# A transformer block on one core: the opening rearranged, empty matmuls as events of the schedule, a new rule table

## Chip, core and metric

The kernel runs on one core of a Trainium2 chip. The metric is the device time of one execution in microseconds (us); less is better. A core has TensorE (PE; its weight loads are listed as PEld), VectorE (DVE), ScalarE (ACT), GpSimd (POOL) and SyncE (SP), which issues most of the DMA transfers.

## The reference, cut to what matters

One block of 2048 tokens with 512 features: modulated layer norm, attention with 32 heads of 16 features, a residual, a second modulated layer norm, a gated FFN with 1792 hidden features, a residual.

```python
mod = (_silu(c) @ w_mod).reshape(c.shape[0], 6, 1, -1)
sa, ca, ga, sb, cb, gb = (mod[:, i].copy() for i in range(6))
h = _layernorm(x) * (1 + ca) + sa
q, k, v = split(h @ wqkv)                       # 32 heads of 16
p = _softmax(einsum('bhqd,bhkd->bhqk', q, k) * 16 ** -0.5)
x = x + ga * ((p @ v) @ wo)
h = _layernorm(x) * (1 + cb) + sb
x = x + gb * (_gelu(h @ w_gate) * (h @ w_up) @ w_down)
```

The scores are 32 x 2048 x 2048 elements, and each of them needs an exponential.

## The kernel before, in words

**The unit of work.** A slot is one bank of scores in PSUM, 128 partitions by 512 columns; the whole softmax has 2048 slots. Four heads are worked on together, on four groups of 32 partitions of TensorE. The queries are cut into seven sets (512, 512, 256, 256, 256, 128 and 128 columns), and a set and a group of four heads are a unit. The variable `pos` counts slots as they are given out.

**Who takes the exponential.** ScalarE takes two or three slots in one instruction (tile `ps_sc` in, tile `E` out, line 399). VectorE takes the others in quads of four slots: it writes bits that are a first approximation of the power of two (`bits`, line 1311: one TENSOR_SCALAR of 512 columns from `ps_sc` per slot), and then makes two factors of them with two masks and one product over 2048 columns each (`power_task`, line 1572). A quad's slots go either one at a time as the third bank beside two of ScalarE's, or three at once with no ScalarE slot beside them ("alone").

**The order of the work** is made when the program is built. A planner keeps a model of every engine's free time and picks what PE does next: scores for the next exponential, products with v, or a piece of side work (projections, output projection, FFN, in a list with due positions). VectorE's work that comes of it waits in a list of tasks, whose length is `backlog()`. Whatever the planner decides becomes the fixed order of instructions on each engine; semaphores do the rest. What steers it are nine numbers for every 64 slots of `pos` (`RULES`, line 69, one row for each stretch, `SEGB = 64`):

- `ready`: how far ahead of PE's modelled time an operation may become ready and still be taken now
- `hole`: how long VectorE may stand empty before a slot until another task is put there
- `back`: the backlog from which no new quad is opened (line 1300)
- `fill`: the columns of PE work in the last 3413 ns below which an empty matmul is put into a gap
- `early`: how late VectorE may be for a quad's slot beside ScalarE's to be accepted (line 1471)
- `alone`: ScalarE's backlog from which three slots go to VectorE alone (line 1453)
- `lag`: the debt from which side work goes first
- `ahead`: the distance in `pos` of the next candidate for a quad
- `side2`: the debt from which side work gets a second PSUM bank, which is asked only from `pos` 1792 on

An empty matmul (`fillers`, line 1407) computes something that is overwritten or adds zeros. It is put in where PE would have a gap of more than 213 ns and its recent work is under `fill`, if one of the possible fillers is ready at once; otherwise the model's clock jumps to the next event.

**The opening** (`prologue`, line 582) is written by hand. DMA brings x, c, the first 1024 columns of w_mod in two parts and the weights of the first heads. The silu of c comes from a Tanh on ScalarE, four tiles of 128 tokens get mean and variance (`ln_stat` on VectorE; tile 1 on ScalarE with accumulating instructions), `ln_rstd` takes eight small VectorE steps for the reciprocal root of all four (tile `nwx`, `nwt`, `rstd`), and the tiles are normed into `dreg`, by VectorE (0 and 2) and ScalarE (1 and 3). `mod_cols` (line 725) computes the modulation as columns: columns 0 to 3 are the shift, 4 to 7 the scale, into `modA`. PE transposes the normed tiles into PSUM, `modulate` multiplies and adds on the way to `hreg`, and q and k of the first heads are projected. This goes in two halves of 256 tokens. k is masked into `kme` and `kmo` (even and odd heads), q is scaled into `qT`, and the first scores follow. Between the steps stand empty matmuls (`warm_up`, line 674).

**After the stream** a tail (line 1664) finishes the last two sets.

Of the kernel before, what the change touches and what calls it, by code (L numbers as in the profile page):

```python
# [6 lines left out]
ACT = mybir.ActivationFunctionType  # L7
ALU = mybir.AluOpType
BF16 = mybir.dt.bfloat16
# [5 lines left out]
P = 128  # L15
# [6 lines left out]
NDC = D // P  # L22
# [15 lines left out]
SC = 2 * CH  # L38
# [14 lines left out]
def WIN(ends):  # L53
# [8 lines left out]
URGENT = 12  # L62
TAILPV = -99
# [431 lines left out]
class _Kernel(_Recorder):  # L495
# [86 lines left out]
    def prologue(self):  # L582
        sp, act, pe, dve, pool = "sp", "act", "pe", "dve", "pool"
# [36 lines left out]
        self.act(self.tcol[:, :], self.scp[:, 0, 0:NDC], ACT.Tanh, scale=0.5)  # L620
        self.ln_stat(0)
# [4 lines left out]
        self.ln_stat(2)  # L626
        self.stt(self.tcol[:, :], self.tcol[:, :], 1.0, self.scp[:, 0, 0:NDC], ALU.add, ALU.mult)
        self.ts(dve, self.sc_bf[:, :], self.tcol[:, :], 0.5, None, ALU.mult)
        self.warm_up(10)
        self.mod_cols(self.scp[:, 1, 0:8], 0, 0, range(4))  # L630
        self.warm_up(8)
        self.ln_stat(3)
        self.ln_rstd(0, 4)
        nb = self.nwt[:, 0:4]
        self.stt(nb, self.mv[:, 0:4, 0], -1.0, self.rstd[:, 0:4], ALU.mult, ALU.mult)
        for t in (0, 1, 2, 3):
            dst = self.tb1[:, 0, t, :]
            if t % 2 == 0:
                self.ln_norm(t, dst)
            else:  # L640
                self.act(dst, self.xs[:, t, :], ACT.Identity, bias=nb[:, t:t + 1], scale=self.rstd[:, t:t + 1])
        self.copy(dve, self.modA[:, 0:4], self.scp[:, 1, 0:4])
        qb = [self.scp[:, 0, 0:256], self.scp[:, 1, 0:256]]
        kb = [self.pv[:, 0:256], self.scp[:, SC - 1, 0:256]]
        own = ((0, 0, 0, 1), (0, 0, 1, 1))
        pts = []
        for h in range(2):
            tb = [self.scp[:, 2 + 2 * h, :].bitcast(BF16), (self.mi if h else self.scp[:, 3, :])[:, :].bitcast(BF16)]
            pts.append([tb[own[h][dc]][:, 256 * dc:256 * dc + 256] for dc in range(NDC)])
            for i in range(2):  # L650
                for dc in range(NDC):
                    self.transpose(pts[h][dc][:, P * i:P * i + P], self.tb1[:, 0, 2 * h + i, P * dc:P * dc + P], self.ident[:, :])
            if h == 0:
                self.mod_cols(self.scp[:, 0, 0:8], 0, 0, range(4, 8))
        self.ts(dve, self.modA[:, 4:8], self.scp[:, 0, 4:8], 1.0, None, ALU.add)
        for h in range(2):
            hs = slice(256 * h, 256 * h + 256)
            for dc in range(NDC):
                self.modulate(act if own[h][dc] else dve, self.hT[:, dc, hs], pts[h][dc], self.modA, dc)
            for n, dc in enumerate((0, 3, 1, 2) if h == 0 else (2, 0, 3, 1)):  # L660
                for out, col in ((qb[h], 0), (kb[h], 512)):
                    self.mm(out, self.wqkv[:, dc, col:col + P], self.hT[:, dc, hs], start=(n == 0), stop=(n == NDC - 1))
        self.ts(dve, self.km[0][:, 0, 0:P], kb[0][:, 0:P], self.rm[:, 0:1], None, ALU.mult)
        self.ts(dve, self.qT[:, 0, 0:256], qb[0], Q_SCALE, None, ALU.mult)
        self.act(self.qT[:, 0, 256:512], qb[1], ACT.Copy, scale=Q_SCALE)
        self.ts(dve, self.km[0][:, 0, P:256], kb[0][:, P:256], self.rm[:, 0:1], None, ALU.mult)
        self.ts(dve, self.km[0][:, 0, 256:512], kb[1], self.rm[:, 0:1], None, ALU.mult)
        for h in range(2):
            self.ts(dve, self.km[1][:, 0, 256 * h:256 * h + 256], kb[h], self.rm[:, 1:2], None, ALU.mult)
# [554 lines left out]
    def stream(self):  # L1224
# [198 lines left out]
        while cg <= group[units[-1]]:  # L1423
# [7 lines left out]
            t = max(self.pe_now(), virt)  # L1431
# [12 lines left out]
            if tq is not None and tq <= t + self.rule.ready:  # L1444
# [41 lines left out]
                n = len(mem)  # L1486
# [345 lines left out]
```

## Time and profile before

| | us |
|---|---|
| median of 3 runs | 817.96 (816.5 to 818.49) |
| the profiled execution | 816.2 |
| its span, first to last instruction | 814.5 |
| ScalarE busy | 792.9 |
| VectorE busy | 753.7 |
| PE busy | 747.7 |

A row of a group reads: line, engine, operation, tile written <- tiles read, shape, count | busy time, mean ns of one | idle time of the engine just before, and what ended it. A row of the timeline reads: start, length, engine, line, operation, tiles, shape, count, and in brackets the idle time before and what ended it. Instructions that follow each other in the same form are merged into one row. A group's mean counts the overlap of neighbours twice, its busy time does not.

### The profile page before, as it was taken

How to read it: one execution, taken by the hardware profiler on the slowest of the kernel's cores; microseconds unless marked ns; L12 is line 12 of the kernel's file. 1: busy time of each engine (PE TensorE's matmuls, PEld its weight loads, DVE VectorE, ACT ScalarE, POOL GpSimd, SP SyncE). 2: the span in 40 equal slices, each digit the busy share in tenths (PEclk: the TensorE clock that was granted, in tenths of full speed). 3: DMA queues.
4: the chain of work that ended last, by engine and by line, in shares of the span. 5: the costliest groups of instructions: out<-in, count | busy, mean ns of one | idle time of the engine just before them, and what ended most of it. 6: DMA issues, size and time to landing. Idle time of an engine off the chain costs nothing.

```text
span 814.5 us, 30576 instructions
## 1 busy us (share of the span) xinstructions
PE 747.7 (92%) x13864; PEld 301.4 (37%) x13864; DVE 753.7 (93%) x1374; ACT 792.9 (97%) x743; POOL 4.6 (1%) x13
## 2 busy tenths in 40 slices
PE   8999999888998988899988989999999998999998
PEld 3333332322222222222233333333544344356565
DVE  7877999999999999999999999999999999889675
ACT  6999999999999999999999999999999999999993
POOL 2000000000000000000000000000000000000000
PEclk9999999999999999999999999999999999999999
DMA  8101000000002211110003212110644143330000
GB/s 285 54 15 23 9 11 9 7 12 10 2 9 63 83 48 36 41 49 21 16 18 99 61 49 58 45 36 10 177 129 135 51 134 101 85 103 9 20 10 14
DMA packets 77356, 43.73 MB, mean 54 GB/s; under 512 B 21285, under 2 KB 75626, under 8 KB 77226
## 3 DMA queue, kind: packets, MB, share of 16 engines
q1 hardware_dynamic: 77224, 41.78, 18.3%
q8 instruction: 108, 1.77, 0.9%
q14 instruction: 22, 0.18, 0.1%
q10 hardware_dynamic: 2, 0.00, 0.0%
HBM read 39.15 MB, written 2.60 MB: 51 GB/s over the span
## 4 chain that ended last, share of the span: by engine, by line
ACT 83%; PE 11%; DVE 5%; DMA 1%; issue 0%; SPq 0%; DVEq 0%
ACT E L399 79%; PE ps_sc L380 5%; PE ps_mi L380 4%; ACT hreg L399 2%; DVE mreg L411 2%; PE ps_pv L380 2%; ACT L399 1%; DVE dreg L411 1%; DMA mreg<-in_w_mod_dram 1%; DVE mreg L403 1%; DVE hreg L403 0%; DVE hreg L420 0%; DVE wo L430 0%; DVE wreg L411 0%; DVE hreg L411 0%
## 5 line engine op out<-in xcount | busy, mean ns | idle before, releaser
L399 ACT ACTIVATE E<-ps_sc 128x1024 bf16<-128x1024 f32 (+1 forms) x702 | 746.4, 1290 | 2.9 <-PE ps_sc L380 2.7
L380 PE MATMUL ps_sc<-qT,kmo 32*128 32x256 bf16 (+2 forms) x1728 | 197.5, 293 | 24.9 <-ACT E L399 21.2
L380 PE MATMUL ps_sc<-qT,kme 32*128 32x256 bf16 (+2 forms) x1728 | 194.4, 293 | 19.8 <-ACT E L399 16.2
L411 DVE TENSOR_SCALAR mreg<-ps_sc 128x512 uint16<-128x512 f32 x252 | 167.9, 683 | 11.4 <-PE ps_sc L380 9.5
L380 PE MATMUL ps_pv<-E,vaug 128*17 128x256 bf16 (+2 forms) x2720 | 150.0, 291 | 1.3 <-DVE osb L427 0.4
L411 DVE TENSOR_SCALAR dreg<-ps_sc 128x512 uint16<-128x512 f32 x160 | 106.9, 684 | 9.5 <-PE ps_sc L380 8.5
L380 PE MATMUL ps_mi<-wreg,mreg 128*32 128x256 bf16 (+2 forms) x1904 | 108.1, 326 | 4.1 <-DVE hreg L403 1.7
L380 PEld LDWEIGHTS ps_sc<-qT,kme 32*128 32x128 bf16 x1728 | 57.1, 92 | 138.5 <-ACT E L399 117.3
L380 PEld LDWEIGHTS ps_sc<-qT,kmo 32*128 32x128 bf16 x1728 | 58.1, 92 | 130.8 <-ACT E L399 113.2
L380 PEld LDWEIGHTS ps_pv<-E,vaug 128*17 128x17 bf16 x2720 | 53.9, 89 | 57.5 <-issue 41.1
L411 DVE TENSOR_SCALAR mreg<-mreg 128x2048 uint16<-128x2048 uint16 x100 | 67.8, 681 | 0.2
L380 PEld LDWEIGHTS ps_mi<-wreg,mreg 128*32 128x32 bf16 (+1 forms) x1904 | 42.2, 95 | 44.8 <-issue 18.5
L380 PE MATMUL ps_pv<-mreg,vaug 128*17 128x256 bf16 (+2 forms) x848 | 50.5, 298 | 2.8 <-DVE mreg L403 1.9
L403 DVE TENSOR_TENSOR mreg<-mreg 128x2048 bf16<-128x2048 bf16 x37 | 45.0, 1215 | 0.1
L403 DVE TENSOR_TENSOR mreg<-dreg,mreg 128x2048 bf16<-128x2048 bf16 x34 | 41.0, 1205 | 0.0
L380 PE MATMUL ps_mi<-hreg,wreg 128*32 128x512 bf16 x480 | 39.4, 385 | 0.8 <-DVE qT L411 0.5
L420 DVE CAST hreg<-ps_mi 128x512 bf16<-128x512 f32 (+1 forms) x49 | 33.0, 673 | 2.3 <-PE ps_mi L380 1.8
L380 PE MATMUL ps_mi<-wo,onorm 128*32 128x512 bf16 x448 | 34.2, 384 | 0.5 <-DVE onorm L403 0.5
L403 DVE TENSOR_TENSOR hreg<-ps_mi,hreg 128x512 bf16<-128x512 f32 x46 | 31.4, 682 | 1.0 <-PE ps_mi L380 0.7
L403 DVE TENSOR_TENSOR dreg<-mreg,dreg 128x2048 bf16<-128x2048 bf16 x26 | 31.4, 1210 | 0.0
L411 DVE TENSOR_SCALAR dreg<-dreg 128x2048 uint16<-128x2048 uint16 x46 | 31.1, 677 | 0.0
L380 PE MATMUL ps_mi<-mreg,hreg 128*32 128x512 bf16 x352 | 29.0, 385 | 0.0
(168 smaller groups left out, 677.6 us busy)
## 6 DMA issues: line engine op xcount, KB each, us to landing
mreg<-in_B_w_up_dram SPq DMA_DIRECT2D x32, 256.0 KB, 2.9
mreg<-in_B_w_gate_dram SPq DMA_DIRECT2D x28, 256.0 KB, 3.2
mreg<-in_B_w_down_dram SPq DMA_DIRECT2D x16, 256.0 KB, 2.7
dreg<-in_B_w_down_dram SPq DMA_DIRECT2D x12, 256.0 KB, 4.9
mreg<-in_w_mod_dram SPq DMA_DIRECT2D x1, 2048.0 KB, 12.1
rb<-scr_rec SPq DMA_DIRECT2D x64, 32.0 KB, 1.8
out_dram<-xs SPq DMA_DIRECT2D x15, 128.0 KB, 1.8
rb<-scr_rec SPq DMA_DIRECT2D x104, 16.0 KB, 1.7
```

What stands on the lines that cost most here:

```text
L380: return self.rec("pe", lambda e: e.matmul(out, lhsT, rhs, start=start, stop=stop, tile_position=tp), [lhsT, rhs, *after], [out], cost=(n, ...
L399: return self.rec("act", lambda e: e.activation(out, in_, func, scale=scale, **kw), rd, wr, cost=self.cost("act", out, [in_], "act") + load)
L403: return self.rec(eng, lambda e: e.tensor_tensor(out, a, b, op), [a, b], [out], cost=self.cost(eng, out, [a, b], "tt"))
L411: return self.rec(eng, lambda e: e.tensor_scalar(out, a, s1, s2, **kw), rd, [out], cost=self.cost(eng, out, [a], "ts") + (60 if len(rd) > ...
L420: return self.rec(eng, lambda e: e.tensor_copy(out, in_), [in_], [out], cost=self.cost(eng, out, [in_], "ts"))
```

## The change

In the opening:

- The statistics of tile 1 on ScalarE come before the Tanh. The three of VectorE come in one go, and the two small steps to the silu stand inside the chain of reciprocal roots.
- Behind the shift columns stand three empty matmuls instead of eight; the scale columns come after the transposes of tile 1 (`MODT = 1`) instead of after those of two tiles in the first half; two empty matmuls come before the projections.
- VectorE norms tiles 0, 1 and 3, ScalarE tile 2. ScalarE copies the shift.
- All four tiles are transposed before they are modulated, in 512 columns instead of two times 256, two on each engine.
- The first 128 key columns are projected apart from the other 384, and ScalarE masks them.

In the stream: of all fillers the one that is ready first is taken, and if none is ready at once, the moment at which it will be is one of the events to which the model's clock can jump. The rule table changes in 18 of its 32 rows: 0, 1, 2, 4, 10 to 14, 16, 18, 20, 23, 25, 26, 27, 30 and 31, in this order below.

```diff
+WARM = (3, 2)
+MODT = 1
 RULES = (
-    (80, 300, 8, 4200, 1536, 400, 1600, 20, 1800),
-    (80, 50, 8, 4200, 1536, 400, 1600, 20, 3200),
-    (60, 200, 7, 3900, 1536, 500, 1900, 24, 700),
+    (60, 200, 7, 3900, 1536, 500, 1600, 24, 700),
+    (80, 50, 10, 4200, 1536, 400, 1600, 20, 3200),
+    (60, 200, 7, 3900, 1536, 500, 1900, 24, 2500),
...
-    (30, 300, 8, 3900, 1536, 500, 2500, 24, 1800),
+    (110, 300, 8, 3900, 1536, 500, 3200, 24, 1800),
...
-    (80, 300, 8, 3600, 1536, 650, 3200, 20, 700),
-    (30, 300, 8, 3900, 1536, 650, 3200, 28, 1024),
-    (30, 200, 8, 3600, 2048, 500, 1300, 20, 1800),
-    (60, 50, 8, 3300, 768, 500, 1900, 12, 3200),
-    (80, 200, 8, 3300, 1536, 850, 3200, 12, 1024),
+    (60, 300, 8, 3600, 1536, 650, 3200, 20, 1800),
+    (30, 300, 8, 3900, 512, 650, 3200, 28, 1024),
+    (30, 50, 8, 3600, 2048, 500, 1300, 20, 3200),
+    (60, 50, 8, 4200, 768, 500, 1900, 16, 3200),
+    (45, 200, 8, 3600, 2048, 1100, 3200, 12, 1024),
...
-    (30, 300, 8, 3300, 1536, 850, 4000, 28, 3200),
+    (30, 300, 8, 3600, 1536, 850, 4000, 28, 3200),
...
-    (15, 200, 8, 3600, 2048, 500, 1900, 24, 2500),
+    (30, 200, 8, 3600, 1536, 850, 4000, 24, 1024),
...
-    (15, 200, 8, 3600, 2048, 500, 1600, 24, 3200),
+    (45, 200, 5, 3600, 2048, 500, 1600, 24, 3200),
...
-    (30, 50, 8, 4200, 768, 500, 3200, 20, 2500),
+    (30, 50, 8, 4200, 768, 500, 1900, 20, 2500),
...
-    (5, 50, 7, 4200, 2560, 850, 1900, 20, 700),
-    (80, 50, 10, 4200, 2560, 650, 1900, 20, 1800),
-    (5, 50, 10, 4200, 2048, 650, 1900, 20, 1800),
+    (110, 50, 7, 4200, 2560, 850, 1900, 20, 700),
+    (80, 50, 10, 4200, 2560, 650, 1600, 20, 2500),
+    (110, 50, 9, 4200, 2560, 850, 2500, 20, 700),
...
-    (80, 50, 10, 4200, 3500, 0, 1900, 20, 1800),
-    (80, 50, 11, 4200, 3500, 1100, 1900, 20, 1800),
+    (80, 50, 9, 3900, 3500, 0, 1900, 20, 1800),
+    (60, 50, 11, 4200, 3500, 300, 1900, 20, 1800),
 )
...
-        self.act(self.tcol[:, :], self.scp[:, 0, 0:NDC], ACT.Tanh, scale=0.5)
-        self.ln_stat(0)
...
-        self.ln_stat(2)
-        self.stt(self.tcol[:, :], ...)
-        self.ts(dve, self.sc_bf[:, :], self.tcol[:, :], 0.5, None, ALU.mult)
+        self.act(self.tcol[:, :], self.scp[:, 0, 0:NDC], ACT.Tanh, scale=0.5)
+        for t in (0, 2, 3):
+            self.ln_stat(t)
         self.warm_up(10)
+        for i in range(self.RSTD):
+            self.ln_rstd_step(0, 4, i)
+            if i == 2:
+                self.stt(self.tcol[:, :], ...)
+            elif i == 4:
+                self.ts(dve, self.sc_bf[:, :], self.tcol[:, :], 0.5, None, ALU.mult)
         self.mod_cols(self.scp[:, 1, 0:8], 0, 0, range(4))
-        self.warm_up(8)
-        self.ln_stat(3)
-        self.ln_rstd(0, 4)
+        self.warm_up(WARM[0])
...
+        for t in range(4):
+            for dc in range(NDC):
+                self.transpose(pts[dc][:, P * t:P * t + P], self.tb1[:, 0, t, P * dc:P * dc + P], self.ident[:, :])
+            if t == MODT:
+                self.mod_cols(self.scp[:, 0, 0:8], 0, 0, range(4, 8))
+        self.warm_up(WARM[1])
+        self.ts(dve, self.modA[:, 4:8], self.scp[:, 0, 4:8], 1.0, None, ALU.add)
...
+        kb = [self.pv[:, 0:P], self.scp[:, SC - 1, 0:512 - P]]
+        ks = [slice(0, P), slice(P, 512)]
+        for dc in range(NDC):
+            self.modulate(act if dc % 2 else dve, self.hT[:, dc, 0:512], pts[dc], self.modA, dc)
+            at = {"start": dc == 0, "stop": dc == NDC - 1}
+            self.mm(kb[0], self.wqkv[:, dc, 512:512 + P], self.hT[:, dc, ks[0]], **at)
+            for h in range(2):
+                self.mm(qb[h], self.wqkv[:, dc, 0:P], self.hT[:, dc, 256 * h:256 * h + 256], **at)
+        for dc in range(NDC):
+            self.mm(kb[1], self.wqkv[:, dc, 512:512 + P], self.hT[:, dc, ks[1]], start=(dc == 0), stop=(dc == NDC - 1))
+        self.act(self.km[0][:, 0, ks[0]], kb[0], ACT.Copy, scale=self.rm[:, 0:1])
         self.ts(dve, self.qT[:, 0, 0:256], qb[0], Q_SCALE, None, ALU.mult)
         self.act(self.qT[:, 0, 256:512], qb[1], ACT.Copy, scale=Q_SCALE)
+        for i, h in ((0, 1), (1, 0), (1, 1)):
+            self.ts(dve, self.km[i][:, 0, ks[h]], kb[h], self.rm[:, i:i + 1], None, ALU.mult)
...
-                fill = next((f for f in fillers() if self.probe(f) <= t + self.rule.ready), None)
+                fill = min([(self.probe(f), i, f) for i, f in enumerate(fillers())], default=None)
+                if fill is not None and fill[0] <= t + self.rule.ready:
+                    fill[2]()
+                    continue
                 if fill is not None:
-                    fill()
-                    continue
+                    nxt = min(nxt, fill[0])
             virt = nxt
```

More of the change, by code (lines that the diff above doesn't have):

```diff
@@ L625, in prologue @@
         self.act(self.mv[:, 1, 1:2], v1[:, 0:1], ACT.Copy, scale=1.0 / D)
-        self.ln_stat(2)
-        self.stt(self.tcol[:, :], self.tcol[:, :], 1.0, self.scp[:, 0, 0:NDC], ALU.add, ALU.mult)
-        self.ts(dve, self.sc_bf[:, :], self.tcol[:, :], 0.5, None, ALU.mult)
+        self.act(self.tcol[:, :], self.scp[:, 0, 0:NDC], ACT.Tanh, scale=0.5)
+        for t in (0, 2, 3):
+            self.ln_stat(t)
         self.warm_up(10)
+        for i in range(self.RSTD):
+            self.ln_rstd_step(0, 4, i)
+            if i == 2:
+                self.stt(self.tcol[:, :], self.tcol[:, :], 1.0, self.scp[:, 0, 0:NDC], ALU.add, ALU.mult)
+            elif i == 4:
+                self.ts(dve, self.sc_bf[:, :], self.tcol[:, :], 0.5, None, ALU.mult)
@@ L630, in prologue @@
         self.mod_cols(self.scp[:, 1, 0:8], 0, 0, range(4))
-        self.warm_up(8)
-        self.ln_stat(3)
-        self.ln_rstd(0, 4)
+        self.warm_up(WARM[0])
         nb = self.nwt[:, 0:4]
         self.stt(nb, self.mv[:, 0:4, 0], -1.0, self.rstd[:, 0:4], ALU.mult, ALU.mult)
-        for t in (0, 1, 2, 3):
+        for t in (2, 0, 1, 3):
             dst = self.tb1[:, 0, t, :]
-            if t % 2 == 0:
+            if t == 2:
+                self.act(dst, self.xs[:, t, :], ACT.Identity, bias=nb[:, t:t + 1], scale=self.rstd[:, t:t + 1])
+            else:
@@ L639, in prologue @@
                 self.ln_norm(t, dst)
-            else:
-                self.act(dst, self.xs[:, t, :], ACT.Identity, bias=nb[:, t:t + 1], scale=self.rstd[:, t:t + 1])
-        self.copy(dve, self.modA[:, 0:4], self.scp[:, 1, 0:4])
-        qb = [self.scp[:, 0, 0:256], self.scp[:, 1, 0:256]]
[L644 to L662, printed above, removed]
@@ L663, in prologue @@
-        self.ts(dve, self.km[0][:, 0, 0:P], kb[0][:, 0:P], self.rm[:, 0:1], None, ALU.mult)
+        self.act(self.modA[:, 0:4], self.scp[:, 1, 0:4], ACT.Copy)
+        tb = [self.scp[:, 2, :].bitcast(BF16), self.scp[:, 4, :].bitcast(BF16)]
+        pts = [tb[dc % 2][:, 512 * (dc // 2):512 * (dc // 2) + 512] for dc in range(NDC)]
+        for t in range(4):
[3 more added lines that the diff above has]
+                self.mod_cols(self.scp[:, 0, 0:8], 0, 0, range(4, 8))
@@ L668, in prologue @@
-        for h in range(2):
-            self.ts(dve, self.km[1][:, 0, 256 * h:256 * h + 256], kb[h], self.rm[:, 1:2], None, ALU.mult)
+        for i, h in ((0, 1), (1, 0), (1, 1)):
+            self.ts(dve, self.km[i][:, 0, ks[h]], kb[h], self.rm[:, i:i + 1], None, ALU.mult)
         self.ln_stat(4)
```

2 lines of the change are left out of this document (removed).

## The prediction

> **What bounds the kernel now.** I read the page first: span, busy time, the chain that ended last.
>
> ```profile
> span 814.5 us, 30576 instructions
> ...
> PE 747.7 (92%) x13864; PEld 301.4 (37%) x13864; DVE 753.7 (93%) x1374; ACT 792.9 (97%) x743; POOL 4.6 (1%) x13
> ...
> ACT 83%; PE 11%; DVE 5%; DMA 1%; issue 0%; SPq 0%; DVEq 0%
> ...
> L399 ACT ACTIVATE E<-ps_sc 128x1024 bf16<-128x1024 f32 (+1 forms) x702 | 746.4, 1290 | 2.9 <-PE ps_sc L380 2.7
> ```
>
> ScalarE holds 83% of the chain, and its exponentials alone are 746.4 of 814.5 us. All waiting ahead of those 702 instructions is 2.9 us, so nothing that merely feeds ScalarE better is worth more than that. Next I cut the span into stages.
>
> ```profile
> 0.00:14.40 14.40, 11.59 (x98) 5.95 (x98) 9.99 (x38) 6.46 (x13) 4.24 (x12) 1.00 0.83 249
> 14.40:43.40 29.00, 26.14 (x409) 9.65 (x412) 24.51 (x76) 28.57 (x25) 0.00 (x0) 1.00 0.32 114
> 43.40:68.70 25.30, 23.84 (x435) 8.87 (x435) 17.74 (x34) 25.18 (x25) 0.31 (x1) 1.00 0.08 23
> 68.70:700.00 631.30, 578.28 (x10048) 208.33 (x10044) 616.60 (x1038) 631.09 (x579) 0.00 (x0) 1.00 0.18 50
> 700.00:794.80 94.80, 91.89 (x2712) 57.13 (x2702) 74.05 (x162) 94.73 (x92) 0.00 (x0) 1.00 0.19 45
> 794.80:814.50 19.70, 15.92 (x199) 11.44 (x187) 10.79 (x32) 6.86 (x13) 0.00 (x0) 0.98 0.05 15
> ```
>
> Columns: length, then busy time of PE, PEld, DVE, ACT and POOL, the granted clock, DMA. The end of the kernel is 14.40 us of opening, 780.4 us in which ScalarE never rests (631.09 of 631.30 us in the long stage), and 19.70 us of tail. The change can move two of these: the moment of the first exponential, and how much of the softmax ScalarE has to do. VectorE does the rest of it, in fours ("quads"). It is 98% busy in the long stage (616.60 of 631.30) but idle 7.56 us of 25.30 in the stage before, and 20.75 of 94.80 in the last. The tail's code is not touched.
>
> **What one quad is worth.** From the groups by shape, for both engines:
>
> ```profile
> L399 ACT ACTIVATE E<-ps_sc 128x1024 bf16<-128x1024 f32 x458 | 450.1, 1149 | 0.6 <-PE ps_sc L380 0.5
> L399 ACT ACTIVATE E<-ps_sc 128x1536 bf16<-128x1536 f32 x240 | 349.2, 1573 | 0.6 <-PE ps_sc L380 0.6
> ...
> L411 DVE TENSOR_SCALAR mreg<-ps_sc 128x512 uint16<-128x512 f32 x252 | 167.9, 683 | 11.4 <-PE ps_sc L380 9.5
> L411 DVE TENSOR_SCALAR dreg<-ps_sc 128x512 uint16<-128x512 f32 x160 | 106.9, 684 | 9.5 <-PE ps_sc L380 8.5
> L411 DVE TENSOR_SCALAR mreg<-mreg 128x2048 uint16<-128x2048 uint16 x100 | 67.8, 681 | 0.2
> L403 DVE TENSOR_TENSOR mreg<-mreg 128x2048 bf16<-128x2048 bf16 x37 | 45.0, 1215 | 0.1
> ```
>
> A third slot of 512 columns costs ScalarE 1573 - 1149 = 0.424 us. ScalarE does 458x2 + 240x3 = 1636 slots, so the whole row of 746.4 us is 0.456 a slot. VectorE does 252 + 160 = 412 slots, 103 quads. One quad more takes 4 slots off ScalarE: 1.70 us by the slope, 1.82 by the average; I take 1.75. It costs VectorE four reads of PSUM at 167.9/252 = 0.666, two masks at 0.678 and one product at 1.216, together 5.2 us. Where VectorE has 5.2 us idle, a quad is a gain.
>
> **The opening, step by step.** The timeline from the vector c to the first exponential:
>
> ```profile
> 1.25 3.17 PE L380 MATMUL ps_mi<-dreg 128*128 128x512 bf16 x7 [1.25 <-DVE dreg L430]
> ...
> 4.55 2.36 PE L380 MATMUL ps_mi<-dreg 128*128 128x512 bf16 x10
> ...
> 4.65 0.17 ACT L399 ACTIVATE tcol<-ps_sc 128x4 f32<-128x4 f32 x1 [2.02 <-PE ps_sc L380]
> ...
> 5.33 0.15 DVE L416 SCALAR_TENSOR_TENSOR tcol<-tcol,ps_sc 128x4 f32<-128x4 f32 x1
> ...
> 5.59 0.68 DVE L442 BATCH_NORM_STATS2 st<-xs 128x6 f32<-128x512 bf16 x1
> ...
> 6.31 0.20 ACT L399 ACTIVATE mv<-nwx 128x1 f32<-128x1 f32 x1
> ...
> 6.62 0.17 DVE L411 TENSOR_SCALAR nwx<-mv 128x4 f32<-128x4 f32 x1
> ...
> 7.77 0.54 PE L380 MATMUL ps_sc<-sc_bf,mreg 128*128 128x1 bf16 x16 [0.86 <-DMA mreg<-in_w_mod_dram]
> ...
> 8.17 1.89 PE L380 MATMUL ps_mi<-dreg 128*128 128x512 bf16 x8
> ...
> 8.21 0.16 DVE L416 SCALAR_TENSOR_TENSOR nwt<-mv,rstd 128x4 f32<-128x4 f32 x1
> ...
> 8.29 0.73 DVE L411 TENSOR_SCALAR dreg<-xs,mv,rstd 128x512 bf16<-128x512 bf16 x2
> ...
> 9.90 0.61 PE L384 MATMUL ps_sc<-ident,dreg 128*128 128x128 bf16 x8
> ...
> 10.34 0.54 PE L380 MATMUL ps_sc<-sc_bf,mreg 128*128 128x1 bf16 x16
> ...
> 10.92 0.16 DVE L411 TENSOR_SCALAR modA<-ps_sc 128x4 f32<-128x4 f32 x1 [1.83 <-PE ps_sc L380]
> ...
> 11.77 1.04 DVE L411 TENSOR_SCALAR hreg<-ps_sc,modA 128x256 bf16<-128x256 bf16 x3
> ...
> 12.72 0.34 DVE L411 TENSOR_SCALAR kme<-ps_pv,rm 128x128 bf16<-128x128 f32 x1
> ...
> 13.44 0.38 ACT L399 ACTIVATE qT<-ps_sc 128x256 bf16<-128x256 f32 x1 [0.78 <-PE ps_sc L380]
> ...
> 13.96 0.59 PE L380 MATMUL ps_sc<-qT,kme 32*128 32x512 bf16 x5 [0.46 <-ACT qT L399]
> ...
> 14.40 10.49 ACT L399 ACTIVATE E<-ps_sc 128x1536 bf16<-128x1536 f32 x9 [0.58 <-PE ps_sc L380]
> ```
>
> *Statistics.* ScalarE now stands 2.02 us waiting for Tanh before it starts tile 1. With Tanh behind the tile's work, that starts at about 3.6 instead of 4.7, and the mean and variance of tile 1 are in about 1 us ahead of the rest. VectorE loses the two small steps in front of the third statistic (5.33 to 5.59, some 0.2 us), so the chain of reciprocal roots starts at about 6.35 instead of 6.62. The two small steps reappear inside the chain; eight steps fill 6.62 to 8.21, 0.2 us each, so they cost between 0 and 0.4, I take 0.2. Norms start about where they did (8.2 against 8.29). Gain: 0.1.
>
> *Matmuls between.* The first modulation columns wait for their weights (DMA, 7.77): unchanged. Behind them stand eight empty matmuls, 1.89 us, that hold the transposes until 9.90 although tile 0 is normed by 8.7 (8.29 and half of 0.73). Three of them are 0.7 us: transposes can start at 8.9. The scale columns now come after two tiles' transposes, at about 9.35. Their weights land in time:
>
> ```profile
> 2.32 0.51 SPq L452 DMA_DIRECT2D mreg<-in_w_mod_dram  x1
> ...
> mreg<-in_w_mod_dram SPq DMA_DIRECT2D x1, 512.0 KB, 6.8
> ```
>
> 2.32 + 6.8 = 9.1. So the scale columns run 9.35 to 9.9 and tiles 2 and 3 are transposed by about 10.5 (0.61 us for eight). Before, the first modulation was held by the scale until 10.92 + 0.16 = 11.1; now it is held by the last transpose, at about 10.6. Gain so far 0.55. The second pair of empty matmuls runs while VectorE and ScalarE modulate; that cover is about 0.5 us wide and without it they would cost 0.4.
>
> *Wide modulations.* Rows of the same operations at other widths:
>
> ```profile
> L411 DVE TENSOR_SCALAR hreg<-ps_mi,modA 128x512 bf16<-128x512 bf16 x12 | 6.0, 539 | 1.8 <-PE ps_mi L384 1.7
> ...
> L399 ACT ACTIVATE dreg<-xs,nwt,rstd 128x512 bf16<-128x512 bf16 x2 | 1.5, 806 | 1.9 <-DVE nwt L416 1.9
> ...
> L399 ACT ACTIVATE hreg<-ps_mi,modA 128x256 bf16<-128x256 bf16 x2 | 1.0, 558 | 0.0
> ```
>
> Four of 512 columns replace eight of 256. VectorE's pair ends at 10.6 + 2 x 0.54 - 0.1 of overlap = 11.6; ScalarE's is between 0.558 + 0.21 = 0.77 and 0.806 each, about 0.68 apart, and ends at 12.05. That is the last one; before, the last ends at 11.77 + 1.04 = 12.8. Gain so far 0.7.
>
> *Projections and first keys.* After the last modulation PE issues the 128-column key part and two query halves, and the second half is done at about 12.6. The price of putting the first 128 keys on ScalarE ahead of the second half of q: between 0 (it ends before the matmul that it would delay) and 0.34 us (VectorE's step of this shape at 12.72); I take 0.1. q is complete at about 13.1 against 13.44 + 0.38 = 13.82, the first scores start at 13.25, the first exponential at 13.7. The remaining 384 key columns are projected while ScalarE writes q, and masked on VectorE by 13.9, a second before the second exponential wants them. [...]
>
> Opening: 0.7 us earlier, between 0.2 (rsqrt chain dearer by 0.4, key step in the way) and 1.1 (none of these).
>
> **The stream.** The opening shifts the start of the stream, but the four key and query steps that VectorE still has there are nearly as long as before, so it gains little time by it; I count that as nothing. Fillers as events: a filler that becomes ready inside a gap is now issued there, and the gap's length is no longer skipped at once. PE is 92% busy and the granted clock 1.00 in every stage to 794.8, so more fillers buy no clock, and one too many costs its length, about 0.24 us (1.89/8), only where ScalarE's buffer of two exponentials has run dry; that is bounded by the 2.9 us of waiting. I take nothing for it.
>
> The rule table decides the number of quads. `side2` is asked only in the last four rules, where it stays as it was, so its edits do nothing. The others pull both ways: rule 1 lets a quad open with 10 steps in VectorE's backlog instead of 8, rules 14, 18 and 27 accept it with VectorE later by 200 to 350 ns, rules 23 and 26 start triples earlier; rule 20 lowers the backlog to 5, 27 and 30 by one, 31 cuts `early` from 1100 to 300, 4, 18 and 27 start triples later. In the long stage VectorE has 14.7 us idle in 631 (the windows above), in pieces; there I let the two signs cancel. Rule 1 acts in the stage 43.4 to 68.7, where idle time is in one place: 7.56 us, less the 0.7 us by which the stage comes earlier, divided by 5.2 is 1.3 quads, 1.3 x 1.75 = 2.3 us. A quad is whole, so one or two.
>
> Sum against the profiled execution: span 814.5 - 0.7 - 2.3 = 811.5. Its own time was 816.2, 1.7 over the span, so 813.2; the median of the runs, 817.96, lies 1.76 above the profiled one, so 815.0.
>
> **Rivals.** *Opening alone.* The backlog was not what held quads back in that stage; VectorE waits there for projections (PE ps_mi), and the count stays at 103. Against: nothing stronger than that rule 1 is the only edit with idle time under it. Time: 817.96 - 0.7 = 817.3, no measurable change.
>
> *Many quads.* The new rules and the last stage's 20.75 idle us hold three to six more: 812.0 down to 806.8. For: the idle time is there. Against: rules 30 and 31 are made stricter in that very stage.
>
> *Fewer quads, slower.* In the long stage rule 20's backlog of 5 and at the end rule 31's `early` turn away quads that were taken, since VectorE there is never short of backlog. Each costs ScalarE 1.75. It decides from two lost net: 817.96 - 0.7 + 3.5 = 820.8; four lost give 824.3. For: 98% busy with a backlog is the state in which a lower limit bites.
>
> *The clock.* In the opening PE loses 5 of 8 and gains 2 empty matmuls. The first seven at the kernel's start ran nearly half as fast (3.17 us for seven) as the next ten (2.36). If the clock fell back like that for some microseconds, half of the transposes (0.61) and the matmuls behind the last modulation (about 0.4) would lie on the path at twice their time: about 0.8 more, which eats the gain, 818.1. Against: the stretch from the three empty matmuls to the two is 1.6 us long (8.9 to 10.5) and has 16 transposes in it. [...]
>
> **Chances.** About 0.3% (2.5 us) is what a measurement of this kernel can tell from no change: 815.5 and 820.4 are the borders. Forecast, one or two quads, 0.44 (of it 0.34 below 815.5, 0.10 just above); many quads 0.16; opening alone 0.19; clock 0.04; fewer quads 0.17. Faster 0.34 + 0.16 = 0.50, same 0.10 + 0.19 + 0.04 = 0.33, slower 0.17. The range goes from four quads more (810.3) to two lost with 0.2 for an opening that gains less (821.0); five or six more, and three or more lost, some 0.13 together, stay outside. The forecast's own range is 813.5 to 816.
>
> **What would show it.** Right: first exponential between 13.3 and 14.2 us; first modulation near 10.6 held by a transpose; 104 or 105 quads (416 or 420 VectorE reads of ps_sc at 0.68); the stage after 43 us with under 5 us of VectorE idle; tail 19.7. Wrong: a first exponential at 14.4 or later, or more than 2 us of ScalarE waiting on PE inside the stream, or 101 quads or fewer.

## The result: 0.2% slower, and the profile after

The median of 22 runs each is 820.14 us after and 818.46 us before; the ratio is 1.0023 (95% interval 1.0012 to 1.0033). One run of after took 1201.72 us, in a slow state; it counts in the median and not in the ratio. The median lies inside the forecast range (810.3 to 821.0) but on the other side of no change: 815.0 and "faster" were forecast. The difference is within the 0.3% that the prediction called no change, but its interval is clear of 1. The profiled execution of after took 821.35 us. The two profiles lie further apart (5.15 us) than the medians (1.7 us): before's was taken from a run 2.3 us under its median, after's from one 1.2 us over. So the profiles are read here for places and the medians for sizes.

From the page of after:

```profile
span 819.6 us, 30628 instructions
...
PE 750.3 (92%) x13887; PEld 303.4 (37%) x13889; DVE 758.4 (93%) x1376; ACT 791.1 (97%) x742; POOL 4.6 (1%) x13
...
ACT 77%; PE 13%; DVE 7%; DMA 2%; issue 1%; SPq 1%; DVEq 0%
...
L401 ACT ACTIVATE E<-ps_sc 128x1024 bf16<-128x1024 f32 (+1 forms) x701 | 745.1, 1295 | 9.1 <-PE ps_sc L382 8.9
```

ScalarE's share of the chain falls from 83% to 77%, although its work falls by only 1.8 us. PE's share grows, and the waits ahead of the exponentials are 9.1 us where they were 2.9. The same stages as in the prediction, cut at after's own first exponential and its own start of the tail (length, then busy time of PE, PEld, DVE, ACT and POOL, granted clock, DMA):

```profile
0.00:13.96 13.96, 12.11 (x93) 5.63 (x94) 8.56 (x31) 6.05 (x14) 4.25 (x12) 1.00 0.79 240
13.96:43.20 29.24, 24.87 (x377) 9.27 (x381) 25.09 (x77) 28.67 (x26) 0.00 (x0) 1.00 0.34 121
43.20:68.50 25.30, 23.83 (x435) 8.85 (x427) 17.75 (x34) 25.21 (x26) 0.31 (x1) 1.00 0.09 24
68.50:700.00 631.50, 580.46 (x10124) 210.57 (x10120) 616.48 (x1037) 631.32 (x579) 0.00 (x0) 1.00 0.18 50
700.00:799.17 99.17, 92.86 (x2640) 56.70 (x2632) 79.40 (x168) 93.02 (x90) 0.00 (x0) 0.98 0.19 43
799.17:819.60 20.43, 16.20 (x246) 12.34 (x247) 11.08 (x33) 6.83 (x13) 0.00 (x0) 0.99 0.05 16
```

The 5.1 us between the spans split by these rows and those of before. Opening: 13.96 against 14.40, -0.44. ScalarE's work in the four middle rows: 778.22 against 779.57, -1.35. Its idle time there: 785.21 - 778.22 = 6.99 against 780.40 - 779.57 = 0.83, so +6.16. Tail: 20.43 against 19.70, +0.73. Of the new idle time all but a fraction is in one row: from 700 us on ScalarE rests 6.15 us (99.17 - 93.02), where it rested 0.07. The groups of both engines:

```profile
L401 ACT ACTIVATE E<-ps_sc 128x1024 bf16<-128x1024 f32 x459 | 450.6, 1154 | 5.5 <-PE ps_sc L382 5.4
L401 ACT ACTIVATE E<-ps_sc 128x1536 bf16<-128x1536 f32 x238 | 346.4, 1581 | 1.9 <-PE ps_sc L382 1.8
...
L413 DVE TENSOR_SCALAR mreg<-ps_sc 128x512 uint16<-128x512 f32 x252 | 168.8, 684 | 8.9 <-PE ps_sc L382 6.8
L413 DVE TENSOR_SCALAR dreg<-ps_sc 128x512 uint16<-128x512 f32 x164 | 109.4, 684 | 7.6 <-PE ps_sc L382 6.1
```

252 + 164 = 416 slots on VectorE: one quad more, as forecast. The waits ahead of exponentials grow from 0.6 and 0.6 us to 5.5 and 1.9, put down to PE.

**The opening after.** Timeline:

```profile
8.43 0.54 PE L382 MATMUL ps_sc<-sc_bf,mreg 128*128 128x1 bf16 x16 [0.35 <-DVE nwt L418]
8.83 0.81 PE L382 MATMUL ps_mi<-dreg 128*128 128x512 bf16 x3
9.47 0.61 PE L386 MATMUL ps_sc<-ident,dreg 128*128 128x128 bf16 x8
...
10.91 1.00 DVE L413 TENSOR_SCALAR hreg<-ps_sc,modA 128x512 bf16<-128x512 bf16 x2 [0.25 <-PE ps_sc L386]
10.97 1.45 ACT L401 ACTIVATE hreg<-ps_sc,modA 128x512 bf16<-128x512 bf16 x2 [1.73 <-PE ps_sc L386]
12.73 0.37 ACT L401 ACTIVATE kme<-ps_pv,rm 128x128 bf16<-128x128 f32 x1 [0.32 <-PE ps_pv L382]
13.00 0.38 ACT L401 ACTIVATE qT<-ps_sc 128x256 bf16<-128x256 f32 x1
...
13.96 2.36 ACT L401 ACTIVATE E<-ps_sc 128x1536 bf16<-128x1536 f32 x2 [0.58 <-PE ps_sc L382]
```

The modulation columns start at 8.43 instead of 7.77, because their weights landed later in this run (8.29 against 7.64 us); over the 17 profiles taken the columns start between 7.65 and 9.05 us. From there to the first exponential it is 5.53 us instead of 6.63 (14.40 - 7.77). So the opening itself is 1.1 us shorter, and the two profiles show only 0.44 of it. Landing earlier helps the new opening only so far: in after_s60 (experiment 3) the weights landed at 6.44 us, and the columns started at 7.91, just behind the silu that now stands in VectorE's chain.

**Where ScalarE stands.** Two places of the timeline after 700 us:

```profile
727.60 1.02 ACT L401 ACTIVATE E<-ps_sc 128x1024 bf16<-128x1024 f32 x1 [1.78 <-PE ps_sc L382]
729.12 1.45 ACT L401 ACTIVATE E<-ps_sc 128x1536 bf16<-128x1536 f32 x1 [0.50 <-PE ps_sc L382]
731.20 8.02 ACT L401 ACTIVATE E<-ps_sc 128x1024 bf16<-128x1024 f32 x8 [0.63 <-PE ps_sc L382]
...
756.24 36.61 ACT L401 ACTIVATE E<-ps_sc 128x1024 bf16<-128x1024 f32 x36 [1.31 <-PE ps_sc L382]
```

And PE and VectorE ahead of the first of them:

```profile
723.79 0.40 PE L382 MATMUL ps_sc<-qT,kme 32*128 32x128 bf16 x12
726.07 1.06 PE L382 MATMUL ps_mi<-wreg,qT 128*32 128x256 bf16 x32 [1.88 <-DVE mreg L413]
...
724.02 0.72 DVE L413 TENSOR_SCALAR wreg<-ps_sc,modB 128x256 bf16<-128x256 bf16 x2
724.66 0.68 DVE L413 TENSOR_SCALAR mreg<-dreg 128x2048 uint16<-128x2048 uint16 x1
```

PE stands for 1.88 us. The releaser that the view infers, VectorE's step on mreg, isn't what held it: these matmuls read wreg and qT, not mreg. In after_shift, a kernel of experiment 2 that issues this stretch in the same order, they start with no idle time, ahead of the end of that step:

```profile
726.08 0.40 PE L382 MATMUL ps_sc<-qT,kme 32*128 32x128 bf16 x12
726.41 1.06 PE L382 MATMUL ps_mi<-wreg,qT 128*32 128x256 bf16 x32
...
726.37 0.68 DVE L413 TENSOR_SCALAR mreg<-dreg 128x2048 uint16<-128x2048 uint16 x1
```

VectorE's two steps on wreg, which the matmuls do read, explain the start of the stall. In after_light, another kernel of experiment 2, the same matmul waits for them alone:

```profile
725.38 1.06 PE L382 MATMUL ps_mi<-wreg,qT 128*32 128x256 bf16 x32 [0.22 <-DVE wreg L413]
```

There the pair on wreg begins at 724.71, so the matmul follows 0.67 us behind it. In after the pair begins at 724.02: the data alone would have held PE until about 724.7, some 0.5 of the 1.88 us. That leaves about 1.4.

What held PE for the rest is found in the queue that carries instructions. From the page's part on DMA queues, then from the DMA view of after at 717 to 724, 721 to 723.5 and 723.5 to 724.7 us:

```profile
q8 instruction: 109, 1.79, 0.9%
```

```profile
DMA  9999999999999999999999999999999999875602
...
q1 hardware_dynamic: 3395, 1.95, 104.4%
```

```profile
q1 hardware_dynamic: 874, 0.77, 101.0%
```

```profile
q8 instruction: 1, 0.02, 5.7%
```

109 packets of 16.4 KB (1.79 MB / 109) stand beside 27,776 matmuls and weight loads: one packet for 27,776 / 109 = 254.8 of them. Below, a block is 256 PE instructions, counted as one packet's, and a border is where one block ends and the next begins. Counted by its place in the program, the matmul at 726.07 comes at a border. So does every other PE gap of over 0.5 us between 715 and 770 us in after, e_r, e_or and after_s60 (kernels of the experiments below). PE ran through the block before it in 3.06 us, from 721.13 on, while the DMA engines were full (101.0%) with the last FFN weights; no instruction packet moved between 721 and 723.5, and it came only when those were through, at 723.58 us. It took 1.09 us, and PE went on 1.4 us after that.

This fits all packets of the traces counted (before, after, e_r, after_s60): a block's packet starts about when PE enters the block before it (median 0.35 to 0.49 us later), and has landed at least 1.2 us before PE enters its own. So in these traces one block was fetched ahead. The packet at whose border PE stood 1.88 us started 723.58 - 721.13 = 2.45 us after PE had entered the block before it. The clock falls behind that stall, in windows cut around it:

```profile
724.00:727.20 3.20, 1.32 (x50) 0.93 (x43) 1.36 (x5) 1.82 (x2) 0.00 (x0) 1.00 0.10 15
727.20:730.60 3.40, 3.40 (x68) 1.98 (x64) 2.30 (x3) 2.47 (x2) 0.00 (x0) 0.50 0.06 18
```

After a stretch in which PE worked 1.32 of 3.20 us, the clock is granted at half for 3.4 us. PE is busy in all of these 3.40 us, so the waits of 0.50 and 0.63 behind the first 1.78 are put down to it. The wait of 1.31 at 756 follows a PE gap of the same size at another border; its packet took 2.16 us, at 752, with the DMA engines 6% busy. That slow packet is no matter of the new order: it is the 97th of its queue, and the 97th takes 1.7 to 3.0 us in 14 of the 17 profiles, three of before's order among them, where the median packet takes 1.0.

### The profile page after: what moved, and what is told of

It is laid out like the page before. It is cut to its first block, busy times and chain, and to the rows that moved or that the text cites. A ratio compares the mean times of both kernels' runs of the same rounds, so it can differ in the third digit from the quotient of the medians.

```text
span 819.6 us, 30628 instructions
## 1 busy us (share of the span) xinstructions
PE 750.3 (92%) x13887; PEld 303.4 (37%) x13889; DVE 758.4 (93%) x1376; ACT 791.1 (97%) x742; POOL 4.6 (1%) x13
## 3 DMA queue, kind: packets, MB, share of 16 engines
q1 hardware_dynamic: 77224, 41.78, 18.5%
q8 instruction: 109, 1.79, 0.9%
## 4 chain that ended last, share of the span: by engine, by line
ACT 77%; PE 13%; DVE 7%; DMA 2%; issue 1%; SPq 1%; DVEq 0%
ACT E L401 73%; PE ps_sc L382 7%; PE ps_mi L382 3%; ACT hreg L401 2%; PE ps_pv L382 2%; DVE dreg L413 1%; ACT L401 1%; DVE st L444 1%; DVE mreg L413 1%; DMA den<-scr_den 1%; SPq L454 1%; DMA rb<-scr_rec 1%; DVE hreg L413 0%; DMA xs<-in_A_x_dram 0%; DVE mreg L405 0%
## 5 line engine op out<-in xcount | busy, mean ns | idle before, releaser
L382 PE MATMUL ps_sc<-qT,kme 32*128 32x256 bf16 (+2 forms) x1728 | 196.6, 295 | 22.2 <-ACT E L401 17.8
L413 DVE TENSOR_SCALAR dreg<-ps_sc 128x512 uint16<-128x512 f32 x164 | 109.4, 684 | 7.6 <-PE ps_sc L382 6.1
L382 PE MATMUL ps_mi<-wreg,mreg 128*32 128x512 bf16 (+2 forms) x1808 | 105.2, 328 | 3.1 <-DVE hreg L422 1.2
L382 PEld LDWEIGHTS ps_mi<-wreg,mreg 128*32 128x32 bf16 (+1 forms) x1808 | 40.0, 95 | 42.3 <-issue 18.7
L382 PE MATMUL ps_pv<-xs,nil 128*17 128x512 bf16 (+1 forms) x464 | 30.3, 339 | 0.0
L405 DVE TENSOR_TENSOR hreg<-ps_mi,hreg 128x512 bf16<-128x512 f32 x43 | 29.4, 684 | 0.8 <-PE ps_mi L382 0.5
```

The source lines that it names most:

```text
L382: return self.rec("pe", lambda e: e.matmul(out, lhsT, rhs, start=start, stop=stop, tile_position=tp), [lhsT, rhs, *after], [out], cost=(n, ...
L405: return self.rec(eng, lambda e: e.tensor_tensor(out, a, b, op), [a, b], [out], cost=self.cost(eng, out, [a, b], "tt"))
L413: return self.rec(eng, lambda e: e.tensor_scalar(out, a, s1, s2, **kw), rd, [out], cost=self.cost(eng, out, [a], "ts") + (60 if len(rd) > ...
```

## The experiments

**1. The three parts taken apart.** Kernels made of before and after in pieces: e_o has the new opening alone, e_r the new rule table alone, e_or both with the old way of issuing fillers, e_fr the new fillers and rules with the old opening.

```
e_o : opening = new   fillers = old   RULES = old
e_r : opening = old   fillers = old   RULES = new
e_or: opening = new   fillers = old   RULES = new
e_fr: opening = old   fillers = new   RULES = new
```

> The kernel before with the new opening alone (old filler choice, old rule table). The planner gives VectorE 400 slots instead of 412 with it. Theory 'count': 12 slots more on ScalarE at 0.43 to 0.46 us are 5.2 to 5.5 us, less 0.4 to 0.7 for the earlier first exponential: 4.5 to 5 us slower than before (ratio 1.0055 to 1.006), first exponential near 13.9 us. Rival 'stalls': what costs time are stalls of PE at block borders of its instructions in the last sets, which the new opening does not bring: then the 5 us are there or not according to ScalarE's idle time between 700 and 800 us, not to the count.

> The kernel before with the new rule table alone. VectorE has 416 slots instead of 412. Theory 'count': one quad more, 1.75 us faster (ratio 0.998). Theory 'stalls': the new rules put other work into the last sets; ScalarE loses 3 to 6 us there to PE, so 1 to 4 us slower (ratio 1.001 to 1.005), with gaps of over 1 us on PE at block borders or behind weight transfers.

> The changed kernel with the old choice of fillers (new opening, new rules). 416 slots. If the fillers as events are what makes the change slower: 2.2 to 2.5 us faster than before (ratio 0.997). If the rules and where they put the late weights are: like the changed kernel, 1 to 3 us slower than before (1.001 to 1.004).

> The changed kernel with the old opening (new fillers, new rules). 412 slots as before, and 242 instructions of three slots instead of 240. Theory 'count': equal to before within 0.5 us (ratio 0.9995 to 1.0005); beside the changed kernel that gives the worth of opening and quad, 2.4 us. Theory 'stalls': slower than before by the gaps in the last sets, 1 to 4 us.

Measured, beside 818.32 of before in the same batch:

| | median us | ratio (95%) | VectorE slots | from modulation columns to first exponential | ScalarE idle after 700 us |
|---|---|---|---|---|---|
| e_o | 829.7 | 1.0140 (1.0114 to 1.0165) | 400 | new, 5.5 to 5.6 | 1.86 |
| e_r | 819.84 | 1.0016 (1.0003 to 1.0029) | 416 | old, 6.63 | 4.55 |
| e_or | 817.58 | 0.9988 (0.9977 to 0.9998) | 416 | new, 5.5 to 5.6 | 2.05 |
| e_fr | 821.31 | 1.0038 (1.0024 to 1.0052) | 412 | old, 6.6 | 4.40 |

The new opening is shorter wherever it stands, but with the old rules the planner takes three quads fewer:

```profile
L413 DVE TENSOR_SCALAR mreg<-ps_sc 128x512 uint16<-128x512 f32 x252 | 169.4, 686 | 18.9 <-PE ps_sc L382 16.3
L413 DVE TENSOR_SCALAR dreg<-ps_sc 128x512 uint16<-128x512 f32 x148 | 99.1, 686 | 8.7 <-PE ps_sc L382 7.3
```

(e_o, groups of VectorE: 252 + 148 = 400.) e_o was expected 4.5 to 5 us slower and is 11.4 slower: against before's profile ScalarE works 6.25 us more in the stream and stands 3.78 more, the tail is 2.04 longer, and the opening gives 0.67 back. So the table does not fit another opening unchanged, and the parts do not add up. e_r and e_fr came out as the theory 'stalls' expected, not as 'count' did. e_or fits neither of its two: its 0.9988 lies between the 0.997 for fillers as the cause and the 1.001 to 1.004 for the rules. e_fr has the new rules and fillers but 412 slots and 4.40 us of idle time, so the idle time is no price of the additional quad.

All three kernels with the new rules stand for 2 us or more after 700 us, with either opening and either fillers; but e_o, with the old rules, stands 1.86 us too. In e_r the largest stall is like the one at 756 in after, at a border, with a slow packet (2.73 us) and the DMA engines 7% busy: PE stops for 1.72 us at 754.7, and in the 4.00 us from 757 on the granted clock is 0.57:

```profile
757.00:761.00 4.00, 4.00 (x72) 1.79 (x72) 0.84 (x2) 3.50 (x3) 0.00 (x0) 0.57 0.07 13
```

**2. Borders moved, or the late weights made small.** after_shift issues each of the first 20 empty matmuls of the opening as four matmuls of 128 columns; the planner keeps its order and costs, and later borders fall 120 instructions earlier in the program. or_shift does the same to 13 of e_or. after_light leaves the order and the borders as they are and brings 16 of 128 partitions of the late weights, so its result is not the block's. The edits, shortened:

```
 def warm_up(self, n):                                   # after_shift
     ...
-        self.mm(self.mi[:, :], self.warm[:, 0:P], self.warm)
+        for x in range(0, 512, P): e.matmul(out[:, x:x + P], w[:, 0:P], w[:, x:x + P], ...)
 ...
-        return lambda: self.dma("sp", dst, src, sem)    # after_light, 11 late parts
+        return lambda: self.rec("sp", lambda e: e.dma_start(dst[0:16], src[0:16]), ...)
```

> The changed kernel, the same order of work on every engine, but 20 of the opening's empty matmuls of 512 columns are issued as four of 128: the same columns, 120 more PE instructions ahead of the stream, so every border of 256 PE instructions falls 120 instructions earlier in the work. Theory 'blocks' (PE stands at such borders when a block is used up before the next has come): the gap of 1.88 us at 724 to 726 goes, another of about 1.1 us appears near 722, the half-clock window after it goes; ScalarE's idle time from 715 to 735 falls from 2.9 to under 1.5 us; 1 to 2 us faster than the changed kernel. Rival 'data' (the first FFN matmul of that set waits for its operands): the gap stays before the same matmul, no change within 0.5 us.

> The changed kernel, the same order, but the eleven late weight transfers (up, last gate, last down) bring 16 of 128 partitions only: the FFN of the last sets computes with old contents there. Theory 'blocks', with the fetch of a block held up by the weights: the border at 721 to 726 then takes 3.5 to 3.8 us instead of 4.94, the gap of 1.88 us shrinks to 0.5 to 0.8, the clock stays full, 2 to 2.5 us faster than the changed kernel; the second gap (754) stays at 1 to 1.7. Rival 'density alone': the border takes 4.9 us with light transfers too, no change.

> New opening and new rules with the old choice of fillers, the same order, 13 of the opening's empty matmuls issued as four: borders 78 instructions earlier. Theory 'blocks': the gap of 1.02 us at 752.4 goes (under 0.4), ScalarE's idle 1.25 us there with it, 1 us faster than without the shift (ratio to before 0.9975). Rival 'data': the same gap before the same matmul, ratio 0.999.

Measured (before 818.05): after_shift 816.7, ratio 0.9986 (0.9976 to 0.9995); after_light 818.65, 1.0002 (0.9991 to 1.0013); or_shift 819.5, 1.0019 (1.0007 to 1.0032). Windows of 720 to 730 and 750 to 758 us, in after, after_shift and after_light:

```profile
720.00:730.00 10.00, 8.12 (x259) 5.64 (x256) 6.61 (x20) 7.72 (x8) 0.00 (x0) 0.86 0.44 120
...
750.00:758.00 8.00, 6.69 (x224) 4.32 (x212) 6.20 (x11) 6.69 (x7) 0.00 (x0) 1.00 0.08 13
```

```profile
720.00:730.00 10.00, 9.40 (x328) 6.76 (x328) 9.22 (x27) 9.96 (x10) 0.00 (x0) 1.00 0.52 142
...
750.00:758.00 8.00, 8.00 (x256) 5.05 (x248) 7.63 (x12) 8.00 (x8) 0.00 (x0) 1.00 0.15 16
```

```profile
720.00:730.00 10.00, 9.48 (x328) 6.82 (x328) 9.24 (x26) 10.00 (x11) 0.00 (x0) 1.00 0.08 15
...
750.00:758.00 8.00, 6.26 (x196) 3.81 (x196) 5.91 (x9) 6.25 (x7) 0.00 (x0) 1.00 0.05 11
```

The first loss needs both: a border there, and full DMA engines. Either edit takes ScalarE from 7.72 back to 9.96 or 10.00 of 10 us, with the clock at 1.00. The sizes were missed: beside after, by the ratios, after_shift is 3.0 us faster (1 to 2 expected) and after_light 1.7 (2 to 2.5 expected), and the gap of about 1.1 us expected near 722 in after_shift is 0.30 us at 724.4. Small weights leave the second loss (6.25 of 8), moved borders don't; it is no matter of the weights. or_shift missed (0.9975 was expected): the gap it aimed at shrank from 1.02 to 0.66 us, but ScalarE then stood 1.46 at 744.5 and 0.38 at 726. Moving borders thus doesn't mend the new order, it draws its stalls again.

**3. Is before as sensitive?** before_s60 and before_s120 move before's borders by 60 and 120 in the same way (10 and 20 matmuls split); after_s60 and or_s120 fill in the places for the new order. before_again is a second profile of the kernel before.

> The kernel before, once more, for a second profile of it: the one shown took 816.2 us where its median is 818.3. If the 2 us are run-to-run differences of the opening's transfers and of the borders, this one shows a first exponential between 14.4 and 15.2 us, 6.6 us behind the first modulation columns in either case, and ScalarE idle for 0 to 2 us between 700 and 800.

> The kernel before, the same order, 10 of the opening's empty matmuls issued as four: borders of 256 PE instructions 60 earlier. Theory 'borders decide 1 to 3 us in either kernel': its median moves by 1 to 3 us from 818.2, to either side; shown at other borders, before is no faster than the changed kernel. Rival 'before lies well by its order': within 0.5 us of before.

> The kernel before with 20 of the empty matmuls issued as four: borders 120 earlier, as in the shifted changed kernel, which took 816.7. Theory 'borders': 1 to 3 us beside 818.2 to either side; without border gaps the changed kernel is 1.1 us (opening) and 1.6 us (quad) ahead of it, so it should be 818 to 821. Rival: 818.2 within 0.5.

> The changed kernel with borders 60 earlier. Theory 'borders': between 816 and 820.5, that is 1 to 3.5 us under 820.1 if the border at 726 leaves the stretch of the late weights, near 820 if it stays there (at 60 it falls to about 723.4, still behind the weights: I expect 819 to 820.5). Rival 'fillers': 820.1 within 0.5 at every border but the one.

> New opening, new rules, old fillers, borders 120 earlier. Unshifted 817.6, 78 earlier 819.5. Theory 'borders': 816 to 820. If fillers as events cost time by themselves, this one is faster than the changed kernel at the same shift (816.7) by 1 us or more; by theory 'borders' it need not be.

Ratios by the distance that the borders were moved:

| order | 0 | 60 | 78 | 120 |
|---|---|---|---|---|
| before | 1 | 1.0002 (0.9990 to 1.0013) | | 1.0006 (0.9992 to 1.0019) |
| after | 1.0023 (1.0012 to 1.0033) | 1.0000 (0.9987 to 1.0012) | | 0.9986 (0.9976 to 0.9995) |
| e_or | 0.9988 (0.9977 to 0.9998) | | 1.0019 (1.0007 to 1.0032) | 1.0011 (0.9999 to 1.0023) |

Before's order stays within 0.06%; the loss of 1 to 3 us expected of it fell. The new order moves over 0.3%, with or without the new fillers: after has the lower time at 120 and e_or at 0. So the fillers as events do not cost time wherever the borders fall. (The places of one row were measured in different batches, each beside before, whose median there was 817.68 to 818.46 us.) after_s60 missed: 819 to 820.5 us was expected, 818.11 measured; its border behind the weights costs PE 0.82 us, not 1.88. ScalarE's idle time after 700 us in before's four profiles is 0.07, 1.48, 0.80 and 0.39 us; in nine with the new rules it is 1.83 to 6.15. before_again took 819.46 us with 3.44 us of idle time in the stream where the first profile had 0.83: the same program, so the stalls also differ from run to run.

**4. The rules from 25 on.** m25 is after with before's rules 25 to 31, which plan the end of the stream; m25_s120 is that with the borders moved; m20 goes back from rule 20 on. A row of the table holds `ready`, `hole`, `back`, `fill`, `lag`, `early`, `alone`, `ahead` and `side2`, in this order, which is not that of the list above; rule 25 differs in `ready` alone.

```
-    (110, 50, 7, 4200, 2560, 850, 1900, 20, 700),     # rule 25, the first of seven
+    (5, 50, 7, 4200, 2560, 850, 1900, 20, 700),
 ...
```

> The changed kernel with rules 25 to 31 of before (from slot 1600 on, about 612 us). VectorE has 412 slots, as before. If rules 25 to 27 make the last sets thin (ScalarE idle 2 to 6 us after 700 us at every border tried): idle time after 700 falls to 0.1 to 1.5 us as in the kernel before, the tail is 19.7 again, and 1.1 us of opening are left over: 0.5 to 1.5 us faster than before (ratio 0.998 to 0.9995). Rival 'the rest of the order' (opening, rules up to 23, fillers): idle after 700 stays at 2 to 6 us, ratio 1.001 to 1.004.

> The same with the borders of 256 PE instructions 120 earlier. If the old rules there make the order robust, as in the kernel before, within 0.1% of the unshifted one; if not, 0.2 to 0.4% beside it.

> The changed kernel with rules 20 to 31 of before. 412 slots. As the one with rules 25 to 31 if rules 25 to 27 are the cause; if rules 20 and 23 are, only this one is back at 0.998 to 0.9995.

Measured (before 818.1): m25 817.59, ratio 0.9993 (0.9980 to 1.0005); m25_s120 818.39, 1.0003 (0.9991 to 1.0014); m20 818.01, 0.9997 (0.9983 to 1.0012). All have 412 slots again: in this opening the additional quad comes with rules 25 to 31 (with the old opening e_fr has them and 412 slots). Idle time after 700 us is 0.82, 1.75 and 1.75, and the tail is back at 19.7, as it is in e_fr: the longer tail goes with the quad. m25 and, just so, m25_s120 came out as expected for rules 25 to 31 as the cause; m20 lies by its interval with m25. The same 10 us as above, in before and in m25:

```profile
720.00:730.00 10.00, 10.00 (x296) 6.60 (x296) 8.95 (x19) 10.00 (x12) 0.00 (x0) 1.00 0.07 12
```

```profile
720.00:730.00 10.00, 9.97 (x298) 6.60 (x290) 8.88 (x20) 10.00 (x11) 0.00 (x0) 1.00 0.16 41
```

Some 590 PE instructions against 656 in after_shift and after_light. With the new rules blocks are used up faster here, and later weights meet them: between 717 and 724 us the data, most of it weights, take 104.4% of the DMA engines in after, 29.2% in before and 58.6% in m25.

## Why the prediction was wrong

**Opening: right in kind, under-sized.** 0.7 us was forecast, 1.1 measured from the modulation columns on. The gain between those columns and the first transpose is 9.47 - 8.43 = 1.04 against 9.90 - 7.77 = 2.13, so 1.09 us: the prediction found it. The rest went as forecast, only sooner: the first modulation, held by a transpose, comes 10.91 - 8.43 = 2.48 us behind the columns, where the working had 10.6 - 7.77 = 2.83; from there to the first exponential it is 3.05 us, against 3.1. So the missing 0.4 lies in the transposes, not in the wide modulations or the key step. That step took 0.37 us. That the clock would halve in the opening did not happen (1.00).

**The quad: right number, wrong place.** One or two were forecast; one came. Rule 1's stage did not change: VectorE idles 25.30 - 17.75 = 7.55 us there, against 7.56. The reason given (backlog 10 instead of 8) was wrong, and the rival's remark, that VectorE waits for projections there, held: 6.7 of the 7.55 us are waits for ps_mi, in before and in after. The quad came with rules 25 to 31, which the prediction let cancel or counted as stricter, so that one came is luck. Worth: 1.35 us of ScalarE's work by the windows, against 1.75.

**Tail: "not touched" was wrong.** It is 0.4 to 0.8 us longer in all kernels with 416 slots, and at 19.7 in those with 412 (e_o, with 400, has 21.7). Its code is the same; what is left over for it isn't. Which step of it grew was not settled.

**The failed step: waiting counted as bounded by what the old order shows.** "I take nothing for it" and "bounded by the 2.9 us of waiting" read the 2.9 us as a property of the kernel. It is one of the order: after's profile has 9.1 us of such waits, 6.15 of its idle time after 700 us. The rule table was read only for what it does to the number of quads; that `ready` goes from 5 to 110 in rules 25 and 27 is not in the prediction, and its sum has no term for the waits of another order. The prediction's test for being wrong, more than 2 us of ScalarE waiting on PE inside the stream, is what happened. None of the rivals named it; "fewer quads" reached the same side by another way, which did not occur. By the medians: 1.7 us = -1.1 opening - 1.35 quad + 0.7 tail + x leaves x = about 3.4 us of additional waiting on average. The profile pair has 6.16, of which the first stall and its half clock are 1.78 + 0.50 + 0.63 = 2.9 and the second 1.31. Of the other 1.9 one wait of 0.92, at 747, stands in after_shift (0.69) and after_light (0.83) too; the rest is in small pieces.

**Shown, and left open.** Shown by moving borders and by shortening the weights: the stall at 724 us, about 1.4 of its 1.88 us, from a block border under full DMA engines. Shown by m25: in the new opening the additional quad and the longer tail come with rules 25 to 31. Without them, and with nothing shifted, most of the idle time is gone (0.82 us, 6.15 with), in one profile of each; but the old choice of fillers alone takes away nearly as much (e_or, 2.05), and moved by 120 after and m25 hardly differ (1.83 and 1.75). So neither the rules nor the fillers alone are the cause of the idle time. That the place of the borders in the order that both make decides over it fits the table of experiment 3, but most of its places are one profile each. Only argued: that denser blocks are why the new order is the more sensitive one. Open: which of the seven rules bring the quad, and why the 97th instruction packet is slow on idle DMA engines.

The fastest versions are after_shift (816.7 us, 0.9986) and e_or (817.58, 0.9988), 1.0 to 1.1 us ahead of before by the ratios, their intervals overlapping. The table of experiment 3 suggests that both owe it to where the borders fall: neither keeps it at another shift.

## What to carry to other kernels

When the busiest engine is at 97%, a new order of the same work is worth its smaller sum of work only if no new stall appears; price its waiting from the densest PE stretch beside the heaviest DMA traffic, not from the old order's waiting. If a few empty instructions move the time as much as the change does, repeat both versions at several offsets before believing a difference of 0.2%. A gain in an opening is to be measured from the landing of its data, not from zero.

## What the runs showed of the hardware

In after the instruction queue brought 109 packets of 16.4 KB, beside 27,776 matmuls and weight loads; the page counts them (0.9%) on the same 16 DMA engines as the data (18.5%). Where a block of 256 was used up in 3.06 us while the data, most of it weights, kept those engines 101.0% busy, the next was entered after 4.94 us and PE stood 1.88 us, about 1.4 of it for the packet. In the four traces counted no block was entered less than 1.2 us after its packet had landed. The view of waits has no name for a packet: it called one such stall a wait for VectorE and left the others to "issue".

The stall of 1.88 us in after was followed by 3.4 us at a granted clock of 0.50; PE had worked 1.32 of the 3.20 us ahead of that. One of 1.72 us in e_r was followed by a clock of 0.57 over 4.00 us. In the window of 750 to 758 us of after, with a stall of 1.31 us in it, the clock was 1.00.
